# Scaling a carried attention state by two plain operations, without a clamp, and rounding later weights later

## The chip, the cores and the metric

The kernel runs on one core of one Trainium2 chip. The metric is device time in microseconds (us) of that core. One more execution is taken with the hardware profiler; its rows are what the views below show. The engines are TensorE (PE, with its weight loads PEld), VectorE (DVE), ScalarE (ACT), GpSimd (POOL) and SyncE (SP), which here only issues DMAs. Every engine works through its own instructions strictly in order.

## What is computed

Three layers in a row, in float32, for 4 batches of 768 positions:

```python
# attention with a decaying state, 8 heads of 48
f = sigmoid(f_logit)
for t in range(768):
    state = f[:, :, t, :, None] * state + k[t] (x) v[t]      # 48 x 48 for each head
    y[t] = q[t] @ state
# gated layer: x = y, 384 wide
h = relu(x @ w_in);  u, v = halves(h);  v = layernorm(v)
x = (u * (w_spatial @ v + b_spatial)) @ w_out
# mixer: first over positions, then over channels
u = x + (relu(x.T @ w_tok1) @ w_tok2).T
out = u + relu(u @ w_ch1) @ w_ch2
```

The weights arrive as 64-bit floats and are rounded to float32 on the chip. Every large product is made of three matmuls on a high and a low part (`mm3`).

## The kernel before

**Attention** is cut into 32 units: 4 batches, 2 halves of 384 positions, 4 pairs of heads. A pair lies on partitions 0 to 47 and 64 to 111. In a unit (`chunked`) DVE scans the decay into `pc` (L227), clamps the three values at the ends of the chunks of 128 from below (L232), inverts them (L233), scans back from them (L234) and scales keys and queries (L237). POOL copies the chunk-end values to `pend` (L230). Each chunk then carries a state: `z` is 112x48 for the pair (L288, L290), and for TensorE it is laid out as two diagonal 48x48 blocks of a 112x112 matrix in one of four buffers `state`, multiplied by the chunk-end decay `pp`. That is done by one instruction per chunk (L277): `z`, repeated twice, times `pp`, times a mask `own` that is 1 in the two blocks. TensorE multiplies it with the queries (L302).

**Rounding.** `round_weight` makes pieces of at most 128x384: a DMA loads the 64-bit words into a `wst` buffer (3 of them), DVE takes two steps (L65, L68), ACT scales (L72), POOL adds (L73), ACT squares (L74), DVE finishes (L78), and a DMA stores the float32 piece in DRAM (L92). The pieces of `w_tok1` (wt1d, 6), `w_tok2` (wt2d, 4), `w_ch1` (wc1d, 12) and `w_ch2` (wc2d, 12) are the list `early`, 34 pieces, staged as 37 steps.

**The order.** `weave` spreads the steps of one list among those of another. The loop over b weaves batch b of the gated layer (`s1`: norm and gate; `s23`: mix and out) with the attention of batch b+1 and with a fifth of `early` at a time. After it come the gated layer of the last batch, with the splitting of the rounded weights (`split_weight`, its subtraction on POOL, L124), and then the mixer. A scheduler moves instructions within each engine by a timeline of its own, so that the order in the program is not the one that is written.

Of the kernel before, what the change touches and what calls it, by code (L numbers as in the profile page):

```python
# [8 lines left out]
F32 = mybir.dt.float32  # L9
# [4 lines left out]
ALU = mybir.AluOpType  # L14
# [4 lines left out]
def tile_kernel(ctx, tc, fkqs, v, w_in, w_sp, b_sp, w_out, w_t1, w_t2, w_c1, w_c2, out):  # L19
    nc = tc.nc  # L20
    B, S, DM = v.shape
    P = 128
    C = 128
    W = S // 2
    D = 48
    H = DM // D
    GAP = 64 - D
    NCW = W // C
    NCH = S // C
    NP = H // 2  # L30
# [10 lines left out]
    LOW = 1e-20  # L41
# [10 lines left out]
    pend = const.tile([P, B * NP, NCH], F32, name="pend")  # L52
# [76 lines left out]
    def staged(pieces):  # L129

        gens = []

        def step(n):
            if n < len(pieces):
                gens.append(pieces[n]())
            for g in gens[max(0, n - 3) : n + 1]:
                next(g, None)

        return [partial(step, n) for n in range(len(pieces) + 3)]

    def weave(main, *fillers):

        for n, m in enumerate(main):
            for fl in fillers:
                for x in fl[len(fl) * n // len(main) : len(fl) * (n + 1) // len(main)]:
                    x()
            m()
# [9 lines left out]
    def body(general):  # L157
# [37 lines left out]
            nc.gpsimd.memset(nhalf, -0.5)  # L195
        first, last = (attp.tile([P, W], F32, name=x) for x in ("first", "last"))
        states = [attp.tile([P, 128], F32, name=f"state{i}") for i in range(4)]
        own = attp.tile([P, 2, D], F32, name="own")
        for t in [first, last, own] + states:
            nc.gpsimd.memset(t, 0.0)  # L200
        for j in range(2):
            nc.gpsimd.memset(own[64 * j : 64 * j + D, j, :], 1.0)
        if general:
            pick = attp.tile([P, D + 128], F32, name="pick")
            nc.gpsimd.memset(pick, 0.0)
# [12 lines left out]
        def chunked(u, b, hf, p, fs, fkq, vt):  # L218
# [8 lines left out]
            nc.vector.tensor_tensor_scan(  # L227
                out=pc, data0=fs[:, :W], data1=first, initial=0.0, op0=ALU.mult, op1=ALU.add
            )
            nc.gpsimd.tensor_copy(pend[:, b * NP + p, n0 : n0 + NCW], pc[:, C - 1 :: C])  # L230
            ends = last[:, C - 1 :: C]
            nc.vector.tensor_scalar(out=ends, in0=pc[:, C - 1 :: C], scalar1=LOW, scalar2=None, op0=ALU.max)  # L232
            nc.vector.reciprocal(ends, ends)  # L233
            nc.vector.tensor_tensor_scan(  # L234
                out=gc[:, ::-1], data0=fs[:, W:0:-1], data1=last[:, ::-1], initial=0.0, op0=ALU.mult, op1=ALU.add
            )
# [33 lines left out]
            for c in range(NCW):  # L270
                n = n0 + c
                if n > 0:
                    zprev = zst[b, p]
                    pp = pend[:, b * NP + p, n - 1 : n]
                    now[c] = states[cnt["state"] % len(states)]
                    cnt["state"] += 1
                    nc.vector.scalar_tensor_tensor(  # L277
                        out=now[c][:112].rearrange("p (j e) -> p j e", j=2)[:, :, :D],
                        in0=zprev[:112].unsqueeze(1).to_broadcast([112, 2, D]),
                        scalar=pp[:112],  # L280
                        in1=own[:112],
                        op0=ALU.mult,
                        op1=ALU.mult,
                    )
                if n < NCH - 1:
                    z = at3.tile([P, D], F32, tag=f"z{p}", name=f"z{u}{c}")
                    if n == 0:
                        nc.vector.tensor_copy(z[:112], pk[:112, c, :])  # L288
                    else:
                        nc.vector.scalar_tensor_tensor(  # L290
                            out=z[:112], in0=zprev[:112], scalar=pp[:112], in1=pk[:112, c, :], op0=ALU.mult, op1=ALU.add
                        )
                    zst[b, p] = z
# [111 lines left out]
        def s1(b, hf):  # L405
            if hf == 0:
                st1[b] = {
                    "vh": vnp.tile([P, NCH, DH], F32R, tag="vh", name=f"vh{b}"),
                    "vl": vnp.tile([P, NCH, DH], F32R, tag="vl", name=f"vl{b}"),
                }  # L410
            d = st1[b]
            d["u", hf] = us = up.tile([P, NJ, W], F32, tag="u", name=f"u{b}{hf}")

            def norm(i):
                xh, xl = xt[b, hf]
                ps = ps_m.tile([P, DH], F32, tag="m", name=f"pv{b}{hf}{i}")
                tsl = slice(i * P, (i + 1) * P)
                mm3(ps, [(xh[:, c, tsl], xl[:, c, tsl], winh[:, c, DH:], winl[:, c, DH:]) for c in range(NK)])
                r = rp.tile([P, DH], F32, tag="r", name=f"r{b}{hf}{i}")
                nc.scalar.activation(r, ps, AF.Relu)  # L420
                bs = smp.tile([P, 6], F32, tag="bs", name=f"bs{b}{hf}{i}")
                nc.vector.bn_stats(out=bs, in_=r)
                mv = smp.tile([P, 2], F32, tag="mv", name=f"mv{b}{hf}{i}")
                nc.vector.bn_aggr(out=mv, in_=bs)
                ve = smp.tile([P, 1], F32, tag="ve", name=f"ve{b}{hf}{i}")
                nc.gpsimd.tensor_scalar(out=ve, in0=mv[:, 1:2], scalar1=1e-6, scalar2=None, op0=ALU.add)
                rs = smp.tile([P, 1], F32, tag="rs", name=f"rs{b}{hf}{i}")
                nc.gpsimd.tensor_tensor(out=rs, in0=ve, in1=nhalf, op=ALU.pow)
                vf = rp.tile([P, DH], F32, tag="vf", name=f"vf{b}{hf}{i}")
                nc.vector.tensor_scalar(  # L430
                    out=vf, in0=r, scalar1=mv[:, 0:1], scalar2=rs, op0=ALU.subtract, op1=ALU.mult
                )
                s = hf * NCW + i
                nc.scalar.copy(d["vh"][:, s, :], vf)
                nc.vector.tensor_tensor(out=d["vl"][:, s, :], in0=vf, in1=f32(d["vh"][:, s, :]), op=ALU.subtract)

            def gate(j):
                xh, xl = xt[b, hf]
                ps = ps_m.tile([P, W], F32, tag="m", name=f"pu{b}{hf}{j}")
                jsl = slice(j * P, (j + 1) * P)  # L440
                mm3(ps, [(winh[:, c, jsl], winl[:, c, jsl], xh[:, c, :], xl[:, c, :]) for c in range(NK)])
                nc.scalar.activation(us[:, j, :], ps, AF.Relu)

            return [partial(norm, i) for i in range(NCW)] + [partial(gate, j) for j in range(NJ)]
# [57 lines left out]
        if not general:  # L502
# [1 line left out]
                kept[name], x = round_weight(wst, src, name)  # L504
                early += x
            early = staged(early)
        part = lambda n: early[len(early) * n // 5 : len(early) * (n + 1) // 5]
        for b in range(B - 1):
            if b:
                weave(s1(b, 0), rest)  # L510
            a, rest = s1(b, 1), []
            m, rest = s23(b)
            steps = att(half(b + 1, 0) + half(b + 1, 1))
            cut = len(steps) * len(a) // len(a + m)
            weave(a, steps[:cut], out_steps if b == 0 else part(2 * b - 1))
            weave(m, steps[cut:], part(2 * b))
        right.close()
        wr2 = ExitStack()
        w2p = wr2.enter_context(tc.tile_pool(name="w2p", bufs=1, side="right"))
# [1 line left out]
        t2h, t2l, st_b = split_weight(w2p, wst, kept["wt2"], "wt2", NT1, S, nc.gpsimd)  # L521
        c1h, c1l, st_c = split_weight(w2p, wst, kept["wc1"], "wc1", NK - 1, DC, nc.gpsimd)
        c1w = [(c1h[:, c, :], c1l[:, c, :]) for c in range(NK - 1)]
        weave(rest + s1(B - 1, 0) + s1(B - 1, 1), staged(st_a + st_b))
        conv = st_c
        mid.close()
        w2q = wr2.enter_context(tc.tile_pool(name="w2q", bufs=1, side="right"))
# [219 lines left out]
```

## Time and profile before

| | |
|---|---|
| median of 3 runs | 828.08 us (825.32 to 829.02) |
| the profiled execution | 828.73 us, its span 827.0 us |
| mean granted TensorE clock | 0.953 of full speed |
| busy share of the span | PE 93%, PEld 86%, DVE 54%, ACT 33%, POOL 29% |

The span runs from the first to the last instruction; 1.7 us of the profiled execution lie around it. A busy share is a mean over stages with different limits, so that each stage has to be read by itself. Durations of neighbours on an engine can overlap, so that what an instruction costs its engine is the time from its start to the start of the next.

### The profile page before, as it was taken

How to read it: one execution, taken by the hardware profiler on the slowest of the kernel's cores; microseconds unless marked ns; L12 is line 12 of the kernel's file. 1: busy time of each engine (PE TensorE's matmuls, PEld its weight loads, DVE VectorE, ACT ScalarE, POOL GpSimd, SP SyncE). 2: the span in 40 equal slices, each digit the busy share in tenths (PEclk: the TensorE clock that was granted, in tenths of full speed). 3: DMA queues.
4: the chain of work that ended last, by engine and by line, in shares of the span. 5: the costliest groups of instructions: out<-in, count | busy, mean ns of one | idle time of the engine just before them, and what ended most of it. 6: DMA issues, size and time to landing. Idle time of an engine off the chain costs nothing.

```text
span 827.0 us, 12669 instructions
## 1 busy us (share of the span) xinstructions
PE 765.1 (93%) x4785; PEld 707.5 (86%) x4785; DVE 443.2 (54%) x916; ACT 274.6 (33%) x590; POOL 240.0 (29%) x290
## 2 busy tenths in 40 slices
PE   3468698999989999999999999999999999999996
PEld 2357577787778888899899999999999999999996
DVE  6997979989898874864464352122122212222211
ACT  4554535445452433323552341112112311111110
POOL 5786835535471112110580340004001210001000
PEclk9659689999989999999999999999999999999999
DMA  7473446575644331120341230002000200000000
GB/s 240 132 219 112 146 127 207 169 255 181 220 132 149 107 104 39 58 82 23 117 134 48 87 115 30 1 1 86 1 29 1 86 1 29 1 1 31 3 28 33
DMA packets 39846, 73.67 MB, mean 89 GB/s; under 512 B 5216, under 2 KB 29664, under 8 KB 39776
## 3 DMA queue, kind: packets, MB, share of 16 engines
q1 hardware_dynamic: 39776, 72.77, 27.7%
q8 instruction: 40, 0.66, 0.3%
q14 instruction: 30, 0.25, 0.1%
HBM read 54.66 MB, written 15.73 MB: 85 GB/s over the span
## 4 chain that ended last, share of the span: by engine, by line
PE 66%; DVE 17%; DMA 6%; issue 5%; POOL 2%; ACT 1%; SPq 1%; DVEq 0%; POOLq 0%; ACTq 0%
PE po L644 18%; PE p L155 8%; PE p L153 8%; PE p L154 8%; PE ps L153 2%; PE ps L155 2%; PE ps L154 2%; PE pa L252 2%; DVE pg L227 2%; PE px L153 2%; PE px L154 2%; PE py L302 2%; PE px L155 2%; PE py L308 1%; DVE state L277 1%
## 5 line engine op out<-in xcount | busy, mean ns | idle before, releaser
L632 DVE SCALAR_TENSOR_TENSOR hl<-p,hh 128x384 fp32r<-128x384 f32 x96 | 53.4, 557 | 189.6 <-ACT hh L631 189.6
L631 ACT ACTIVATE hh<-p 128x384 fp32r<-128x384 f32 x96 | 47.1, 492 | 198.1 <-PE p L155 198.1
L644 PE MATMUL po<-hl,wc2h 128*128 128x384 f32 x288 | 97.2, 338 | 0.0
L644 PE MATMUL po<-hh,wc2l 128*128 128x384 f32 x288 | 96.7, 336 | 0.0
L655 POOL TENSOR_TENSOR us<-uh,ul 128x384 f32<-128x384 f32 x24 | 24.4, 1027 | 233.4 <-DVE ul L615 216.1
L644 PE MATMUL po<-hh,wc2h 128*128 128x384 f32 x288 | 75.0, 336 | 0.0
L153 PE MATMUL ps<-wsph,vh 128*128 128x384 f32 x192 | 66.6, 348 | 0.0
L155 PE MATMUL ps<-wsph,vl 128*128 128x384 f32 x192 | 65.9, 345 | 0.0
L154 PE MATMUL ps<-wspl,vh 128*128 128x384 f32 x192 | 65.6, 342 | 0.0
L155 PE MATMUL p<-uh,wc1l 128*128 128x384 f32 x192 | 65.0, 338 | 0.0
L154 PE MATMUL p<-ul,wc1h 128*128 128x384 f32 x192 | 64.7, 337 | 0.0
L153 PE MATMUL p<-uh,wc1h 128*128 128x384 f32 x192 | 64.2, 338 | 0.0
L257 POOL TENSOR_SCALAR_AFFINE_SELECT am<-am 128x384 f32<-128x384 f32 x64 | 42.9, 686 | 58.9 <-ACT am L256 58.7
L644 PEld LDWEIGHTS po<-hl,wc2h 128*128 128x128 f32 x288 | 54.1, 188 | 0.0
L644 PEld LDWEIGHTS po<-hh,wc2l 128*128 128x128 f32 x288 | 54.1, 188 | 0.0
L644 PEld LDWEIGHTS po<-hh,wc2h 128*128 128x128 f32 x288 | 52.3, 188 | 0.0
L302 PE MATMUL py<-fkq,state 112*112 112x128 f32 x160 | 37.4, 332 | 13.4 <-DVE state L277 10.9
L302 PEld LDWEIGHTS py<-fkq,state 112*112 112x112 f32 x160 | 26.6, 201 | 23.0 <-DVE state L277 15.9
L252 PE MATMUL pa<-fkq 48*128 48x128 f32 x384 | 40.7, 328 | 0.0
L615 DVE TENSOR_TENSOR ul<-p,uh 128x384 fp32r<-128x384 f32 x24 | 13.4, 557 | 47.6 <-ACT uh L614 47.6
L252 PEld LDWEIGHTS pa<-fkq 48*128 48x128 f32 x384 | 30.7, 215 | 9.0 <-issue 5.1
L153 PE MATMUL pu<-xh,winh 128*128 128x384 f32 x96 | 34.9, 364 | 3.6 <-ACT r L420 2.8
(407 smaller groups left out, 1944.2 us busy)
## 6 DMA issues: line engine op xcount, KB each, us to landing
fkq<-in_fkq SPq DMA_DIRECT2D x31, 576.0 KB, 4.5
vt<-in_v SPq DMA_DIRECT2D x8, 576.0 KB, 6.2
x1d<-xs SPq DMA_DIRECT2D x24, 192.0 KB, 2.0
xf<-x1d SPq DMA_DIRECT2D x12, 384.0 KB, 4.1
out<-ot SPq DMA_DIRECT2D x24, 192.0 KB, 2.5
wspsa<-in_w_sp SPq DMA_DIRECT2D x12, 192.0 KB, 3.2
wc1d<-wc1da SPq DMA_DIRECT2D x12, 192.0 KB, 2.0
wc2d<-wc2da SPq DMA_DIRECT2D x12, 192.0 KB, 2.1
```

The costliest lines, as they stand in the source:

```text
L153: nc.tensor.matmul(ps, lh, rh, start=first and i == 0, stop=False, **kw)
L154: nc.tensor.matmul(ps, lh, rl, start=False, stop=False, **kw)
L155: nc.tensor.matmul(ps, ll, rh, start=False, stop=i == n - 1, **kw)
L227: nc.vector.tensor_tensor_scan(out=pc, data0=fs[:, :W], data1=first, initial=0.0, op0=ALU.mult, op1=ALU.add)
L252: nc.tensor.matmul(pa[j][:, c, :], ki[64 * j : 64 * j + D, sl], qi[64 * j : 64 * j + D, sl], start=True, stop=True)
L257: nc.gpsimd.affine_select(out=am[j], in_=am[j], compare_op=ALU.is_ge, fill=0.0, base=0, pattern=[[0, NCW], [1, C]], channel_multiplier=-1,)
L302: nc.tensor.matmul(py[:112, c, :], now[c][:112, :112], qi[:112, c * C : (c + 1) * C], start=c == 0, stop=False, skip_group_check=True,)
L615: nc.vector.tensor_tensor(out=ul[:, c, tsl], in0=ps, in1=f32(uh[:, c, tsl]), op=ALU.subtract)
L631: nc.scalar.activation(hh, ps, AF.Relu)
L632: nc.vector.scalar_tensor_tensor(out=hl, in0=ps, scalar=0.0, in1=f32(hh), op0=ALU.max, op1=ALU.subtract)
L644: nc.tensor.matmul(po[c], l[:, ft, csl], r, start=ft == 0 and x == 0, stop=ft == NF - 1 and x == 2)
L655: nc.gpsimd.tensor_tensor(out=us[c], in0=f32(uh[:, c, tsl]), in1=f32(ul[:, c, tsl]), op=ALU.add)
```

## The change

Three things are changed. The state is laid out by two `tensor_scalar` instructions, one for each 48x48 block, in place of one over 112x2x48 with a mask; the mask `own` goes. The clamp (L232) goes, and the reciprocal reads the scan directly. The copy to `pend` is made by ACT instead of POOL. And `early` is dealt out in fourteenths: nothing in the round of b=0, 2/14 and 3/14 in that of b=1, 2/14, 2/14 and 3/14 in that of b=2, and the last 2/14 beside the gated layer of the last batch.

```diff
-        own = attp.tile([P, 2, D], F32, name="own")
-        for t in [first, last, own] + states:
+        for t in [first, last] + states:
             nc.gpsimd.memset(t, 0.0)
-        for j in range(2):
-            nc.gpsimd.memset(own[64 * j : 64 * j + D, j, :], 1.0)
...
-            nc.gpsimd.tensor_copy(pend[:, b * NP + p, n0 : n0 + NCW], pc[:, C - 1 :: C])
-            ends = last[:, C - 1 :: C]
-            nc.vector.tensor_scalar(out=ends, in0=pc[:, C - 1 :: C], scalar1=LOW, scalar2=None, op0=ALU.max)
-            nc.vector.reciprocal(ends, ends)
+            nc.scalar.copy(pend[:, b * NP + p, n0 : n0 + NCW], pc[:, C - 1 :: C])
+            nc.vector.reciprocal(last[:, C - 1 :: C], pc[:, C - 1 :: C])
...
-                    nc.vector.scalar_tensor_tensor(
-                        out=now[c][:112].rearrange("p (j e) -> p j e", j=2)[:, :, :D],
-                        in0=zprev[:112].unsqueeze(1).to_broadcast([112, 2, D]),
-                        scalar=pp[:112],
-                        in1=own[:112],
-                        op0=ALU.mult,
-                        op1=ALU.mult,
-                    )
+                    for j in range(2):
+                        r = slice(64 * j, 64 * j + D)
+                        nc.vector.tensor_scalar(
+                            out=now[c][r, r], in0=zprev[r], scalar1=pp[r], scalar2=None, op0=ALU.mult
+                        )
...
-        part = lambda n: early[len(early) * n // 5 : len(early) * (n + 1) // 5]
+        part = lambda n, m: early[len(early) * n // 14 : len(early) * m // 14]
         for b in range(B - 1):
             if b:
-                weave(s1(b, 0), rest)
+                weave(s1(b, 0), rest, part(7 * b - 9, 7 * b - 7) if b > 1 else [])
...
-            weave(a, steps[:cut], out_steps if b == 0 else part(2 * b - 1))
-            weave(m, steps[cut:], part(2 * b))
+            weave(a, steps[:cut], out_steps if b == 0 else part(7 * b - 7, 7 * b - 5))
+            weave(m, steps[cut:], part(7 * b - 5, 7 * b - 2) if b else [])
...
-        weave(rest + s1(B - 1, 0) + s1(B - 1, 1), staged(st_a + st_b))
+        weave(rest + s1(B - 1, 0) + s1(B - 1, 1), staged(st_a + st_b), part(12, 14))
```

**On DVE.** These rows stand where unit 103 (batch 1, first half, last pair) carries its state and unit 111 is scanned; a scan is listed as SCALAR_TENSOR_TENSOR writing `pg`. Before:

```order
L277 SCALAR_TENSOR_TENSOR state2_126<-z1030_1369,pend_64,own_128 112x2x48
L290 SCALAR_TENSOR_TENSOR z1031_1372<-z1030_1369,pend_64,pk103_1361 112x48
L226 MEMSET fs111_1429 128x4
L467 TENSOR_TENSOR gl000_1292<-g000_1288,gh000_1291 128x384
L68 SCALAR_TENSOR_TENSOR wc1da0768_2355<-wc1d0768st_2356,wc1da0768_2355 128x384
L78 SCALAR_TENSOR_TENSOR wc1da0384_2311<-wc1d0384st_2312,wc1da0384_2311 128x384
L277 SCALAR_TENSOR_TENSOR state3_127<-z1031_1372,pend_64,own_128 112x2x48
L290 SCALAR_TENSOR_TENSOR z1032_1375<-z1031_1372,pend_64,pk103_1361 112x48
L227 SCALAR_TENSOR_TENSOR pg111_1431<-fs111_1429,first_122 128x384
```

And after the change, with the lines of the changed program (L274 is the new state, L282 the `z` that was L290, L228 the reciprocal):

```order
L274 TENSOR_SCALAR state2_126<-z1030_1375,pend_64 48x48 x2
L282 SCALAR_TENSOR_TENSOR z1031_1379<-z1030_1375,pend_64,pk103_1367 112x48
L224 SCALAR_TENSOR_TENSOR pg111_1439<-fs111_1437,first_122 128x384
L65 TENSOR_SCALAR wc1da0768_2987<-wc1d0768st_2988 128x384
L454 TENSOR_TENSOR g002_1428<-ps002_1409,bb_495 128x384
L459 TENSOR_TENSOR gl001_1364<-g001_1360,gh001_1363 128x384
L274 TENSOR_SCALAR state3_127<-z1031_1379,pend_64 48x48 x2
L282 SCALAR_TENSOR_TENSOR z1032_1383<-z1031_1379,pend_64,pk103_1367 112x48
L228 RECIPROCAL last_123<-pg111_1439 128x3
```

Two state instructions stand together in place of one, the clamp is gone, and the weight pieces stand a little further back.

**On POOL and ACT.** The copy of the chunk ends of unit 111 stood here on POOL, in front of rounding steps:

```order
L257 AFFINE_SELECT am1100_1447<-am1100_1447 128x384
L257 AFFINE_SELECT am1101_1448<-am1101_1448 128x384
L230 COPY pend_64<-pg111_1431 128x3
L73 TENSOR_TENSOR wc1da01152_2412<-wc1da01152_2412,wc1d01152st_2413 128x384
L73 TENSOR_TENSOR wc1da10_2506<-wc1da10_2506,wc1d10st_2507 128x384
```

It now stands on ACT, with a rounding step, the copies of unit 110's scores (`am`) and more behind it (lines of the changed program):

```order
L458 CAST gh001_1363<-g001_1360 128x384
L74 ACTIVATE wc1d0384st_2911<-wc1d0384st_2911 128x384
L240 COPY kn110_1450<-pt110_1447 128x224
L227 COPY pend_64<-pg111_1439 128x3
L72 ACTIVATE wc1d01152st_3051<-wc1d01152st_3051 128x384
L251 COPY am1100_1454<-pa1100_1452 128x384
L251 COPY am1101_1455<-pa1101_1453 128x384
```

What follows the copy on ACT now waits for the scan of unit 111 as the copy does.

**The last pieces.** On POOL beside the gated layer of the last batch there are three rounding steps of `w_ch2` after the change that were all done earlier before (`wt1l` and `wt2l` are the low parts of split weights):

```order
L124 TENSOR_TENSOR wt1l_4253<-wt1sa30_4378,wt1h_4252 128x256
L73 TENSOR_TENSOR wc2da90_4306<-wc2da90_4306,wc2d90st_4307 128x384
L418 TENSOR_SCALAR ve302_4406<-mv302_4404 128x1
L124 TENSOR_TENSOR wt1l_4253<-wt1sa40_4416,wt1h_4252 128x256
L420 TENSOR_TENSOR rs302_4408<-ve302_4406,nhalf_63 128x1
L124 TENSOR_TENSOR wt1l_4253<-wt1sa50_4431,wt1h_4252 128x256
L73 TENSOR_TENSOR wc2da100_4387<-wc2da100_4387,wc2d100st_4388 128x384
```

The third of them (wc2da110) stands five rows on. In both programs the other 31 pieces stand on DVE ahead of the scan of unit 210 (batch 2, second half), where before all 34 did.

## Rows read from the trace of the kernel before

**Rows 1.** The page: busy tenths in 40 slices of the span, granted clock.

```profile
PE   3468698999989999999999999999999999999996
DVE  6997979989898874864464352122122212222211
PEclk9659689999989999999999999999999999999999
```

**Rows 2.** Busy time by stretch: stretch, length, each engine's busy time (instructions), clock, DMA.

```profile
0.00:250.00 250.00, 196.68 (x1300) 160.81 (x1301) 224.16 (x470) 122.51 (x273) 141.46 (x172) 0.85 0.57 179
250.00:390.00 140.00, 139.66 (x1032) 121.66 (x1031) 94.55 (x232) 47.70 (x106) 23.88 (x49) 1.00 0.25 80
390.00:470.00 80.00, 78.77 (x440) 76.07 (x439) 35.88 (x58) 32.35 (x69) 32.86 (x37) 1.00 0.30 93
470.00:827.00 357.00, 349.96 (x2018) 348.95 (x2017) 88.62 (x157) 72.01 (x143) 41.77 (x34) 1.00 0.09 29
```

**Rows 3.** Waits of TensorE, 250 to 390 us: total, times, longest.

```profile
PE py L302 <- DVE state L277: 0.3, 1, 0.3
```

**Rows 4.** Waits of TensorE, 390 to 470 us.

```profile
PE pu L153 <- ACT r L420: 1.2, 1, 1.2
```

**Rows 5.** Waits of all engines, 0 to 250 us.

```profile
POOL pend L230 <- DVE pg L227: 23.3, 12, 4.1
...
PEld py L302 <- DVE state L277: 15.2, 17, 2.6
...
DVE first L225 <- ACT fs L369: 12.4, 4, 4.0
```

**Rows 6.** Line 277 (state) alone, by stretch: its time on DVE (instructions).

```profile
0.00:250.00 250.00, 23.20 (x46) 0.85 0.57 179
250.00:390.00 140.00, 11.29 (x34) 1.00 0.25 80
```

**Rows 7.** Line 232 (clamp) alone, by stretch, on DVE.

```profile
0.00:250.00 250.00, 8.22 (x20) 0.85 0.57 179
250.00:390.00 140.00, 2.10 (x12) 1.00 0.25 80
```

**Rows 8.** Line 230 (copy to pend) alone, first stretch, on POOL.

```profile
0.00:250.00 250.00, 8.17 (x20) 0.85 0.57 179
```

**Rows 9.** Lines 65, 68, 78 (DVE) and 73 (POOL) alone, first stretch.

```profile
0.00:250.00 250.00, 21.96 (x47) 0.85 0.57 179
...
0.00:250.00 250.00, 26.47 (x47) 0.85 0.57 179
...
0.00:250.00 250.00, 29.86 (x47) 0.85 0.57 179
...
0.00:250.00 250.00, 56.63 (x47) 0.85 0.57 179
```

**Rows 10.** DVE by line, 250 to 390 us: shapes, count, busy us, mean ns, idle before.

```profile
L290 DVE SCALAR_TENSOR_TENSOR z<-z,pend,pk 112x48 f32<-112x48 f32 x26 | 6.7, 256 | 0.2 <-PE pk L267 0.2
...
L288 DVE COPY z<-pk 112x48 f32<-112x48 f32 x5 | 1.0, 198 | 0.5 <-PE pk L267 0.5
```

**Rows 11.** Single lines: duration ns min/median/max, first and last start.

```profile
L232 DVE TENSOR_SCALAR last<-pg x32: 154/169/993, 5.3 to 369.6; 128x3 f32<-128x3 f32 x32
...
L65 DVE TENSOR_SCALAR wc1da<-wc1d00st x1: 346/346/346, 139.4 to 139.4; 128x384 uint32<-128x384 uint32 x1
```

**Rows 12.** Timeline of DVE around 122 us: start us, duration us, what.

```profile
121.50 0.31 DVE L277 SCALAR_TENSOR_TENSOR state<-z,pend,own 112x96 f32<-112x96 f32 x1
121.73 0.25 DVE L290 SCALAR_TENSOR_TENSOR z<-z,pend,pk 112x48 f32<-112x48 f32 x1
121.90 0.41 DVE L78 SCALAR_TENSOR_TENSOR wt1da<-wt1d40st,wt1da 128x256 f32<-128x256 f32 x1
```

**Rows 13.** Timeline of POOL and DVE around 147 us.

```profile
146.69 1.48 POOL L73 TENSOR_TENSOR wc1da<-wc1da,wc1d0384st 128x384 uint32<-128x384 uint32 x1 [4.67 <-ACT wc1d0768st L72]
...
147.22 1.07 DVE L277 SCALAR_TENSOR_TENSOR state<-z,pend,own 112x96 f32<-112x96 f32 x1
148.21 0.25 DVE L290 SCALAR_TENSOR_TENSOR z<-z,pend,pk 112x48 f32<-112x48 f32 x1
```

**Rows 14.** ACT by line, 250 to 390 us.

```profile
L245 ACT COPY kn<-pt 128x224 f32<-128x224 f32 (+1 forms) x12 | 4.5, 378 | 5.9 <-PE pt L243 5.9
```

## The prediction

> **What bounds the kernel now.** Read first the page's 40 slices [rows 1]. TensorE is full from about the thirteenth slice on; before that it has holes, its granted clock is often below full, and it is DVE that stands at 9 tenths. So the kernel has two regimes, and an edit on DVE counts only in the first. The busy times by stretch give it numbers [rows 2]: from 0 to 250 us DVE is busy 224.16 of 250 us and TensorE 196.68; from 250 to 390 us it is the other way round, TensorE 139.66 of 140 and DVE 94.55; from 390 us to the end TensorE is busy for 428.73 of 437 us. TensorE's waits agree: between 250 and 390 us its matmuls wait 0.3 us in all for another engine [rows 3], between 390 and 470 us 1.2 us [rows 4], while in the first stretch its weight loads alone wait 15.2 us for the carried state [rows 5]. What the change does to DVE's time before 250 us is therefore what it does to the kernel, times about 0.9 (224.16 of 250), because DVE idles for the other tenth. Behind 250 us an edit on DVE has 45 us of cover.
>
> One more thing must be seen in that first stretch: DVE and POOL hinder each other. The same state instruction takes 11.29/34 = 0.33 us in the second stretch, where POOL is busy 23.88 of 140 us, and 23.20/46 = 0.50 us in the first, where POOL is busy 141.46 of 250 [rows 2, 6]. One of 1.07 us ends as POOL's instruction ends, and the `z` behind it, which reads PSUM, takes its usual 0.25 [rows 13]. So 46 x 0.17 = 7.9 us are lost on state instructions to POOL.
>
> **The change, part by part (first stretch).** What an instruction costs DVE is from its start to the next start. State at 121.50 and `z` at 121.73: 0.23 us for a duration of 0.31. An independent neighbour starts 0.08 before its predecessor ends, here and at 121.90 [rows 12].
>
> *State.* No row shows a 48x48 `tensor_scalar`. The one over 128x3 takes 0.154 at its shortest, the one over 128x384 takes 0.346 undisturbed [rows 11]: 0.0005 us a column, so 0.177 for 48. Neither has a scalar read from memory; `z` has one (and a second input) and takes 0.256, where the copy of the same 112x48 takes 0.198 [rows 10]: 0.058 more. Estimate 0.235, less the overlap 0.155, twice 0.31 against 0.23 now: +0.08 x 46 = **+3.7 us**. Bounds: each as short as the 128x3 one, 0.075 from start to start, gives 0.15 for two, -3.7 us; no overlap at all gives 0.47 for two, +11.0 us. I take the overlapped value, since the nearest row, state and `z`, both reading the same `z`, overlaps.
>
> *Its collisions with POOL.* Two instructions can each meet POOL; the second loses between nothing and again 7.9 us. If the two overlap, POOL has little room between them, and a first one that waited starts just when POOL has finished. I take half, **+4.0**.
>
> *Clamp.* 8.22 us for 20 instructions [rows 7], many of which collide with the copy on POOL that starts at the same scan's end. Where something independent follows, 0.08 of each was overlapped (at most 1.6 in all); where the reciprocal follows, the gap goes too. **-8.0**, between -6.6 and -8.9.
>
> *Rounding.* In the order the pieces move little: 31 of 34 still stand ahead of unit 210's scan, which DVE reaches near the end of the first stretch. Three leave it. A piece costs DVE (21.96 + 26.47 + 29.86)/47 = 1.67 us, less three overlaps 1.43 [rows 9]: **-4.3**. Their DMAs, loads and stores on SP, and their ACT and POOL steps go with them.
>
> *The copy to pend.* POOL is rid of 8.17 us here [rows 8] and of three rounding steps of 56.63/47 = 1.2 us. A POOL instruction can hold DVE for its own length at most, so the copies give between 0 and -8.2; the share that collides is some quarter (the state loses 0.17 against a mean POOL step of 141.46/172 = 0.82), **-2.0**. ACT takes 20 copies of less than 0.38 us, the time of a 128x224 copy [rows 14]; it is idle for half the stretch [rows 2], so its time costs nothing. If ACT were full, it would be up to 7.6 us.
>
> Sum on DVE: 3.7 + 4.0 - 8.0 - 4.3 - 2.0 = **-6.6**, times 0.9 **-5.9 us** of the kernel.
>
> **Behind 250 us.** 34 states add 34 x 0.08 = 2.7 us to a DVE with 45 us to spare, and 12 clamps give 2.1 back [rows 7]: nothing. The three late pieces put 3 x 1.2 = 3.6 us on a POOL that is busy 32.86 of the 80 us from 390 us on [rows 2], in front of the norms' small POOL steps, for which DVE and then TensorE wait. TensorE waits 1.2 us there now [rows 4]; I add +0.4, bounds 0 and 3.6. The mask's memsets at the start lie beside the first loads: nothing.
>
> The profiled execution took 828.73 us, 0.65 above the median and inside the spread of the runs: 828.73 - 5.9 + 0.4 = **823.2 us**.
>
> **Rivals.**
>
> *The two halves do not overlap.* All DVE instructions of this trace start at partition 0; the second half of the new state starts at 64 and the `z` behind it at 0 again. If a change of the start partition makes DVE finish what is under way, the 0.08 of overlap is lost twice for each state: 46 x 0.16 = +7.4. DVE then gains nothing, 3.7 + 7.4 + 4.0 - 14.3 = +0.8, times 0.9 and with the 0.4: **829.8 us**. No row speaks for or against it. The Trainium skill, "VectorE: DVE Perf Modes", section "Two Vector instructions with no wait between them", states just such a rule for this chip: an instruction that starts in another group of 32 partitions than the one ahead is held until every earlier one is finished. By that rule the sum would end at this rival's time and not at mine; no run here shows it yet.
>
> *ACT becomes the queue that stands still (slower).* POOL waited 23.3 us in the first stretch for scans that its copy needs [rows 5]. This wait moves to ACT, whose sigmoids, score copies and evictions stand behind it, as the order of unit 111 shows. If half of it comes back as idle time on DVE, 11.6 us are added: 823.2 + 11.6 = **834.8 us**. Against it: ACT has half its time free, and DVE's order puts other work between a scan and what needs the ACT work behind the copy. It decides when DVE's waits for ACT, now 12.4 us for the sigmoids [rows 5], rise by more than 5.5 us; by 9.0 more it is slower by half a per cent.
>
> *The state is no dearer under POOL.* The second half never collides (no +4.0) and the copies had all stood in DVE's way (-8.2, not -2.0): -16.8 x 0.9 + 0.4, **814.0 us**. For it: clamp and copy start together at each scan's end.
>
> *The gain is given back behind 390 us*, where the late pieces delay the norms, and so TensorE, by their whole 3.6 us: 828.73 - 5.9 + 3.6 = 826.4 us. For it: POOL's order there; against it: TensorE has matmuls of the batch before to run.
>
> **How the numbers follow.** My case 0.38, no overlap 0.27, ACT 0.18, cheap state 0.13, given back 0.04. A run of this kernel tells apart about half a per cent, 4.1 us, so from 823.9 to 832.2 us counts as the same. My case sits just beyond that line: I give 0.24 of it to faster and 0.14 to the same. No overlap: 0.02 faster, 0.20 the same, 0.05 slower. ACT: 0.04 the same, 0.14 slower. Cheap state: 0.13 faster. Given back: 0.03 the same, 0.01 faster. Together 0.40 faster, 0.41 the same, 0.19 slower. The likeliest single case remains mine, alone within 819 to 827 us. The range for all, 815 to 834 us, cuts off about half of the cheap state and half of ACT.
>
> **What would show it.** In the profile after: the new state line's duration (0.235 by me) and, in the timeline, whether its second half and the `z` behind it start 0.08 before or at the end of what is ahead; the state's time per chunk in the first stretch (now 0.50 us; by me two of 0.24 and 0.17 to 0.34 of collisions); DVE's waits for `fs` and ACT's for `pg`; three `wc2da` steps after 390 us and TensorE's waits there; and where TensorE becomes full, about 6 us earlier. I am wrong if that point does not move, or if it moves and the time does not.

## The result: slower by 1.1 per cent

The changed kernel takes 835.53 us (median of 4 runs, 835.12 to 836.25) against 827.15 for the kernel before, run on the same chip: ratio 1.0111, 95% interval 1.0094 to 1.0127. That is above the forecast range. Its profiled execution took 836.25 us, its span 834.2. Of all executions below, one stands apart: one of the six of e2 took 1470.31 us, and e2's median and ratio are those of the other five.

The page of the changed kernel, the slices of [rows 1]:

```profile
PE   3469698898989999999989999999999999999996
...
DVE  6998988999989774675555252222122312122211
...
PEclk9999688988989999999999999999999999999999
```

Busy time by stretch after the change, columns as in [rows 2]:

```profile
0.00:250.00 250.00, 199.09 (x1280) 163.81 (x1281) 227.94 (x484) 123.89 (x286) 130.13 (x144) 0.90 0.56 176
250.00:390.00 140.00, 138.98 (x1017) 120.90 (x1017) 101.50 (x254) 50.62 (x120) 20.92 (x38) 1.00 0.26 81
390.00:470.00 80.00, 76.55 (x432) 73.35 (x431) 39.82 (x66) 31.20 (x65) 34.30 (x37) 1.00 0.29 91
```

The two regimes stand as before. POOL has 11.3 us less to do in the first stretch, but DVE is busy for 227.94 us and not for less. The waits there, after the change, answer to [rows 5]:

```profile
ACT pend L227 <- DVE pg L224: 20.0, 15, 3.9
PEld py L294 <- DVE state L274: 19.0, 19, 2.9
...
DVE first L222 <- ACT fs L361: 8.6, 3, 3.9
```

TensorE's loads wait longer for the state (19.0 us against 15.2), DVE less for the sigmoids (8.6 against 12.4). The new state line alone, by stretch, answers to [rows 6]:

```profile
0.00:250.00 250.00, 36.58 (x92) 0.90 0.56 176
250.00:390.00 140.00, 17.85 (x68) 1.00 0.26 81
```

The timeline of DVE after the change, in a window that holds only the first half of a state, and then in a wider one in which the halves are merged into one row (x2):

```profile
121.75 0.39 DVE L68 SCALAR_TENSOR_TENSOR wt1da<-wt1d50st,wt1da 128x256 uint32<-128x256 uint32 x1
122.06 0.23 DVE L274 TENSOR_SCALAR state<-z,pend 48x48 f32<-48x48 f32 x1
...
122.06 0.49 DVE L274 TENSOR_SCALAR state<-z,pend 48x48 f32<-48x48 f32 x2
122.58 0.27 DVE L282 SCALAR_TENSOR_TENSOR z<-z,pend,pk 112x48 f32<-112x48 f32 x1
122.76 0.82 DVE L422 TENSOR_SCALAR vf<-r,mv,rs 128x512 f32<-128x512 f32 x1
```

The first half starts 0.08 us before the row ahead ends. The second can't have: a half lasts 0.23 and the two last 0.49, so that nothing overlaps and some 0.01 to 0.03 us lies empty between them. `z` starts 0.03 after the second. Behind `z` an overlap of 0.09 is back (122.76 against 122.85). From state to `z` it is 0.52 us, where it was 0.23 [rows 12]. To the nanosecond of the trace, wherever the two halves stand next to each other (76 times) the second starts 0.014 to 0.016 us after the end of the first, and a `z` that stands behind them mostly 0.032 after the end of the second.

TensorE waits in the stretch from 390 to 470 us, after the change, answer to [rows 4]; the second row had no like before:

```profile
PE pu L153 <- ACT r L412: 2.1, 1, 2.1
...
PE ps L153 <- ACT u L434: 1.3, 1, 1.3
```

**A mark in the program.** One small matmul, `row`, stands on TensorE between the third batch's last product and the norm of the last batch; its start tells where the change's first part ends. Before and after:

```profile
394.31 0.27 PE L544 MATMUL row<-ident,least 128*1 128x128 f32 x1
```

```profile
398.65 0.27 PE L536 MATMUL row<-ident,least 128*1 128x128 f32 x1
```

Taken from the time of the profiled execution it leaves 828.73 - 394.31 = 434.42 us behind the mark before, and 836.25 - 398.65 = 437.60 after: of 7.52 us lost, 4.34 are lost ahead of the mark and 3.18 behind it. Between the medians 8.4 us are lost (835.53 - 827.15).

### The profile page after: what moved, and what is told of

Read it like the earlier page. It is cut to its first block, busy times and chain, and to the rows that moved or that the text cites. A ratio compares the mean times of both kernels' runs of the same rounds, so it can differ in the third digit from the quotient of the medians.

```text
span 834.2 us, 12686 instructions
## 1 busy us (share of the span) xinstructions
PE 771.4 (92%) x4785; PEld 713.7 (86%) x4785; DVE 459.8 (55%) x964; ACT 281.1 (34%) x622; POOL 229.5 (28%) x255
## 4 chain that ended last, share of the span: by engine, by line
PE 66%; DVE 17%; DMA 7%; issue 5%; SPq 2%; POOL 1%; ACT 1%; DVEq 0%; ACTq 0%; POOLq 0%
PE po L636 18%; PE p L155 8%; PE p L153 8%; PE p L154 8%; PE ps L153 3%; DVE state L274 3%; PE ps L155 3%; PE ps L154 3%; DVE pg L224 2%; DMA fkq<-in_fkq 2%; PE px L153 2%; PE px L155 2%; PE py L300 2%; PE pa L247 2%; PE px L154 1%
## 5 line engine op out<-in xcount | busy, mean ns | idle before, releaser
L252 POOL TENSOR_SCALAR_AFFINE_SELECT am<-am 128x384 f32<-128x384 f32 x64 | 47.5, 758 | 111.2 <-ACT am L251 110.8
L274 DVE TENSOR_SCALAR state<-z,pend 48x48 f32<-48x48 f32 x160 | 54.4, 340 | 1.9
L247 PE MATMUL pa<-fkq 48*128 48x128 f32 x384 | 43.6, 334 | 0.0
L247 PEld LDWEIGHTS pa<-fkq 48*128 48x128 f32 x384 | 32.8, 219 | 9.9 <-issue 5.8
L153 PEld LDWEIGHTS ps<-wsph,vh 128*128 128x128 f32 x192 | 36.9, 192 | 3.8 <-ACT u L434 1.7
```

What stands on the lines that cost most here:

```text
L153: nc.tensor.matmul(ps, lh, rh, start=first and i == 0, stop=False, **kw)
L247: nc.tensor.matmul(pa[j][:, c, :], ki[64 * j : 64 * j + D, sl], qi[64 * j : 64 * j + D, sl], start=True, stop=True)
L252: nc.gpsimd.affine_select(out=am[j], in_=am[j], compare_op=ALU.is_ge, fill=0.0, base=0, pattern=[[0, NCW], [1, C]], channel_multiplier=-1,)
L274: nc.vector.tensor_scalar(out=now[c][r, r], in0=zprev[r], scalar1=pp[r], scalar2=None, op0=ALU.mult)
```

## The experiments

Each ratio is to runs of the kernel before on the same chip, whose median was 825.96 to 827.32 us. The mark is that of the profiled execution, the last column the profiled time less the mark. The profiled execution of before stands 1.6 us above the median of its runs here, so that the marks can be read to about 2 us. The granted clock does not make such differences: of the 103 executions of the kernel before that stand beside e1 to e18, the 27 with a mean clock below 0.967 have a median of 827.1 us, the others of 826.4. Behind the mark it is 434.1 to 436.1 us in all kernels without late rounding pieces, and 437.0 to 438.4 in all six that have them.

| kernel | median | ratio (interval) | mark | behind it |
|---|---|---|---|---|
| before | | | 394.31 | 434.42 |
| changed | 835.53 | 1.0111 (1.0094 to 1.0127) | 398.65 | 437.60 |
| e1 changed, one state operation | 830.03 | 1.0047 (1.0030 to 1.0065) | 391.02 | 438.40 |
| e2 before, two state operations | 840.21 | 1.0168 (1.0147 to 1.0189) | 405.27 | 435.93 |
| e3 before, rounding later | 827.35 | 1.0024 (1.0008 to 1.0041) | 389.19 | 437.04 |
| e4 before, no clamp, copy on ACT | 828.74 | 1.0029 (1.0015 to 1.0043) | 392.60 | 436.08 |
| e5 changed, halves from partition 0 | 827.41 | 1.0011 (0.9995 to 1.0028) | 392.17 | 437.01 |
| e6 before, no clamp | 825.93 | 1.0003 (0.9985 to 1.0020) | 391.25 | 434.38 |
| e7 before, copy on ACT | 833.74 | 1.0090 (1.0067 to 1.0114) | 398.35 | 435.95 |
| e8 e3 without late pieces | 826.69 | 1.0002 (0.9987 to 1.0017) | 392.07 | 434.58 |
| e9 e7, copy behind `kn` | 830.98 | 1.0053 (1.0032 to 1.0074) | 393.87 | 434.81 |
| e10 e9, no clamp | 832.74 | 1.0062 (1.0041 to 1.0083) | 398.62 | 434.99 |
| e11 e10, rounding later | 831.95 | 1.0064 (1.0043 to 1.0085) | 394.01 | 437.96 |
| e12 changed, copy on POOL | 835.55 | 1.0105 (1.0084 to 1.0127) | 399.92 | 437.51 |
| e13 before, fkq loads by POOL | 832.55 | 1.0071 (1.0048 to 1.0094) | 399.64 | 434.35 |
| e14 before, fkq loads by ACT | 824.38 | 0.9980 (0.9965 to 0.9995) | 389.29 | 434.11 |
| e15 e13, no clamp | 833.28 | 1.0075 (1.0050 to 1.0101) | 399.56 | 434.08 |
| e16 e13, copy on ACT | 839.16 | 1.0145 (1.0119 to 1.0171) | 404.86 | 434.40 |
| e17 e8, fkq loads by ACT | 825.21 | 0.9989 (0.9973 to 1.0005) | 390.99 | 434.38 |
| e18 e5, no late pieces, loads by ACT | 832.91 | 1.0075 (1.0053 to 1.0098) | 398.59 | 434.94 |

### The parts of the change: e1 to e4

Theory: the two halves don't overlap. Rival: ACT's queue stands still at the copy. Each part alone, or all but the state:

```diff
# e1, to the changed kernel (e2, to the kernel before: the reverse)
-                        nc.vector.tensor_scalar(
-                            out=now[c][r, r], in0=zprev[r], scalar1=pp[r], scalar2=None, op0=ALU.mult
-                        )
+                    nc.vector.scalar_tensor_tensor(
+                        out=now[c][:112].rearrange("p (j e) -> p j e", j=2)[:, :, :D],
...
# e3, to the kernel before: part(n, m) and its four uses as in the change
-        part = lambda n: early[len(early) * n // 5 : len(early) * (n + 1) // 5]
+        part = lambda n, m: early[len(early) * n // 14 : len(early) * m // 14]
...
# e4, to the kernel before
-            nc.gpsimd.tensor_copy(pend[:, b * NP + p, n0 : n0 + NCW], pc[:, C - 1 :: C])
-            ends = last[:, C - 1 :: C]
-            nc.vector.tensor_scalar(out=ends, in0=pc[:, C - 1 :: C], scalar1=LOW, scalar2=None, op0=ALU.max)
-            nc.vector.reciprocal(ends, ends)
+            nc.scalar.copy(pend[:, b * NP + p, n0 : n0 + NCW], pc[:, C - 1 :: C])
+            nc.vector.reciprocal(last[:, C - 1 :: C], pc[:, C - 1 :: C])
```

> The changed kernel with the state put back to one instruction with the mask; clamp gone, copy on ACT and rounding as changed. Theory 1 (the change of start partition keeps the two halves and the z behind them apart: 0.29 us more per state on DVE, 46 states before 250 us): about 823 us, faster than before by 0.5%, TensorE's last-batch mix earlier by some 10 us than in the changed kernel. Theory 2 (the copy on ACT holds its queue up): still 833 us or more. Theory 3 (the late rounding pieces): the 2.6 us that the changed kernel loses between 390 and 430 us are lost here too, whatever the rest does.

> The kernel before with nothing but the two-instruction state. Theory 1: DVE is charged 46 x 0.29 = 13 us before 250 us and nothing is given back, so 836 to 840 us, slower than the changed kernel or equal to it. Theory 2: within 0.3% of before. Theory 3: the same, within 0.3% of before.

> The kernel before with nothing but the rounding pieces dealt out later. Theory 1: three pieces leave the first stretch, about 4 us saved there, and the stretch behind 390 us may take some back: 823 to 828 us. Theory 3 (late pieces stand in POOL's and ACT's queues beside the last gated layer): TensorE loses 2.6 us between 390 and 430 us, net 827 to 830 us.

> The kernel before with the clamp gone and the copy of the chunk ends on ACT, one state instruction, rounding as before. Theory 1: DVE is rid of 8 us before 250 us: 820 to 823 us. Theory 2 (ACT's queue stands still for the scans): 831 us or more, with DVE's waits for the sigmoids above the 12.4 us of before.

The state alone costs 1.68 per cent, 14 us: more than the whole change. The state line of e2, by stretch:

```profile
0.00:250.00 250.00, 37.60 (x88) 0.94 0.55 174
250.00:390.00 140.00, 17.90 (x68) 1.00 0.28 88
```

The rounding and the two edits at the scan's ends, which were to gain, lose a quarter of a per cent each. The rounding's mark comes 5.1 us earlier, but behind the mark it loses 2.6. Of the 5.1, some 3.7 are scatter: the profiled execution of before stands 2.6 above the median of e3's chip, that of e3 1.1 below its own.

e1 takes 830 us where theory 1 had 823. These two edits do add up: 0.24 and 0.29 per cent, and 0.47 for both in e1. It is the state that does not: 14 us alone, and in the changed kernel only 835.53 - 830.03 = 5.5 us. Why it is cheaper there is not shown.

### The start partition alone: e5

```diff
+            for j in range(2):
+                r = slice(64 * j, 64 * j + D)
+                nc.scalar.copy(half_ends[r, j, b * NP + p, n0 : n0 + NCW], pc[r, C - 1 :: C])
...
-                            out=now[c][r, r], in0=zprev[r], scalar1=pp[r], scalar2=None, op0=ALU.mult
+                            out=now[c][:112, 64 * j : 64 * j + D], in0=zprev[:112],
+                            scalar1=half_ends[:112, j, b * NP + p, n - 1 : n], scalar2=None, op0=ALU.mult,
```

Two operations still, of 48 columns each, but both over 112 partitions from partition 0; `half_ends` holds the chunk ends with zeros in the other head's rows.

> The changed kernel with each of the two state instructions over 112 partitions from partition 0 (112x48), scaled by a column of chunk ends that holds zeros for the other half; ACT makes two more small copies per unit for these columns. As many state instructions with as many columns as in the changed kernel, but none changes the start partition. Theory 1 (the change of start partition): neighbours overlap by 0.08 us again, state to state about 0.16 us instead of 0.25, the pair and z 0.2 us cheaper per state, some 9 us before 250 us: 826 to 830 us, near the version with one state instruction (830 us). Rival 1b (it is the number of instructions, not where they start): 835 us as the changed kernel, and 0.25 us from start to start.

It is back at the time of before, 8.1 us below the changed kernel, with two copies more for ACT in each unit. Up to one and the same instruction (TensorE's first transpose for unit 212: batch 2, second half, third pair) the changed kernel and then e5 show

```profile
0.00:280.10 280.10, 229.19 (x1503) 190.45 (x1504) 253.22 (x548) 133.54 (x310) 134.34 (x150) 0.91 0.54 169
```

```profile
0.00:274.00 274.00, 225.50 (x1500) 187.21 (x1501) 243.03 (x544) 140.84 (x358) 135.32 (x151) 0.93 0.55 173
```

so 10.2 us less on DVE, and the point 6.1 earlier. The timeline of DVE in e5:

```profile
252.35 0.39 DVE L277 TENSOR_SCALAR state<-z,half_ends 112x48 f32<-112x48 f32 x2
252.66 0.25 DVE L286 SCALAR_TENSOR_TENSOR z<-z,pend,pk 112x48 f32<-112x48 f32 x1
252.95 0.40 DVE L277 TENSOR_SCALAR state<-z,half_ends 112x48 f32<-112x48 f32 x2
```

The two last 0.39 us together, and `z` starts 0.08 before they end: 0.31 from state to `z`, where the changed kernel has 0.52. The state line of e5, by stretch:

```profile
0.00:250.00 250.00, 30.84 (x94) 0.92 0.57 181
250.00:390.00 140.00, 14.38 (x66) 1.00 0.23 71
```

Busy time counts a stretch in which two overlap once: so a half comes to 0.218 us in the second stretch here and to 0.263 in the changed kernel. Single ones are as long in both, as the view of the one line shows (shortest, median and longest in ns), of e5 and of the changed kernel:

```profile
L277 DVE TENSOR_SCALAR state<-z,half_ends x160: 211/242/1067, 17.8 to 382.6; 112x48 f32<-112x48 f32 x160
```

```profile
L274 DVE TENSOR_SCALAR state<-z,pend x160: 207/247/1034, 17.2 to 389.4; 48x48 f32<-48x48 f32 x160
```

The start partition is shown as the cause of the 0.21 us. In e5 the second operation overlaps the first by 0.076 to 0.092 us wherever the two stand next to each other (79 times), though both write one tile there too. Nor is it the height: in the changed kernel the first half, of 48 partitions, overlaps the row of 128 ahead of it by 0.08. How much of the 8.1 us of the kernel it makes is less sharp. The program's order on DVE differs between the two kernels in other places as well, and e5 is 2.6 us faster than e1, whose single state operation costs DVE 0.08 us less.

### Clamp and copy apart, and the rounding without its late pieces: e6 to e8

e6 takes the clamp away and e7 puts the copy on ACT, each alone in the kernel before. e8 is e3 with the last 2/14 moved up:

```diff
-            weave(m, steps[cut:], part(7 * b - 5, 7 * b - 2) if b else [])
+            weave(m, steps[cut:], part(7 * b - 5, 7 * b - 2 if b < 2 else 14) if b else [])
...
-        weave(rest + s1(B - 1, 0) + s1(B - 1, 1), staged(st_a + st_b), part(12, 14))
+        weave(rest + s1(B - 1, 0) + s1(B - 1, 1), staged(st_a + st_b))
```

> The kernel before without the clamp, the copy of the chunk ends still on POOL, nothing else. If the 8 us of the clamp on DVE are real: 819 to 822 us. Rival 2b (the clamp only stood where POOL's copy held DVE anyway, so the wait moves on to the next instruction that needs the shared way to SBUF): 825 to 828 us, and the scan back or its neighbours are longer by what the clamp no longer waits.

> The kernel before with nothing but the copy of the chunk ends moved from POOL to ACT. Theory 2 (ACT's queue stands still for the scans): 830 to 834 us, so that with the clamp's saving the two come to the 829 us that they measured together. Rival: 824 to 827 us, POOL being rid of 8 us.

> The kernel before with the rounding dealt out as changed but for the last 2/14, which go into the round of b=2 with the rest; all 34 pieces then stand ahead of unit 210's scan again. Theory 3 (three pieces less before 250 us give some 3 us and cost some 2.6 us behind 390 us): both vanish, 825 to 828 us, and TensorE loses nothing between 390 and 430 us. Rival: the gain came from the spacing of the pieces, not from the three that leave, and without the late ones it is 823 us.

Taken from the kernel before, the clamp is worth nothing that can be measured. DVE is indeed rid of it: up to the first transpose for unit 212 the kernel before and e6 show

```profile
0.00:277.90 277.90, 224.24 (x1516) 184.59 (x1516) 246.46 (x528) 130.35 (x291) 145.62 (x180) 0.86 0.55 173
```

```profile
0.00:273.10 273.10, 223.58 (x1500) 186.48 (x1501) 241.29 (x500) 131.45 (x290) 149.65 (x179) 0.94 0.55 176
```

so 246.46 - 241.29 = 5.2 us less on DVE and the point 4.8 earlier; at the mark 3.1 are left, and of these 1.6 are the scatter of the profiled execution of before. With the copy on ACT right behind the scan the clamp is worth something: e4 is e7 without it and takes 5.0 us less. The copy alone costs 0.9 per cent. ACT's wait for the scan and a new wait of DVE stand in e7's first stretch:

```profile
ACT pend L230 <- DVE pg L227: 11.9, 12, 2.2
...
DVE first L225 <- ACT fs L369: 9.2, 4, 3.9
...
DVE state L277 <- PE py L302: 7.0, 2, 5.2
```

DVE's wait for the sigmoids is no longer than before; what is new are 7.0 us in which it waits for TensorE to give a state buffer back.

Moved up, the late pieces cost nothing behind the mark: 434.58 us there, against 437.04 in e3. TensorE's waits from 390 to 470 us in e3, and then in e8:

```profile
PE ps L153 <- ACT u L442: 2.0, 1, 2.0
...
PE pu L153 <- ACT r L420: 1.5, 1, 1.5
```

```profile
PE pu L153 <- ACT r L420: 1.2, 1, 1.2
```

The wait of the last batch's mix is there only with the late pieces, in five of the six kernels that have them; e5 lacks it and still takes 437.01 us behind the mark, so that the wait does not explain all of this cost. And e8's mark is 2.9 us later than e3's.

### Is it ACT's standing wait: e9 to e12

In e9 the copy stands behind that of `kn`, whose zero column is its bias, so that what it waits for is long done. e10 is e9 without the clamp, e11 adds the rounding as changed; e12 is the changed kernel with the copy back on POOL.

```diff
-            nc.gpsimd.tensor_copy(pend[:, b * NP + p, n0 : n0 + NCW], pc[:, C - 1 :: C])
...
             nc.scalar.copy(kn[:, :ncs, :], pt[:, :ncs, :])
+            nc.scalar.activation(
+                pend[:, b * NP + p, n0 : n0 + NCW], pc[:, C - 1 :: C], AF.Identity, bias=kn[:, 0, D : D + 1]
+            )
```

> The kernel before with the copy of the chunk ends on ACT, but with a zero column of the transposed keys (kn) as its bias, so that it stands right behind the copy of kn and never waits for the scan. Theory 2 (on ACT the copy's wait for the scan holds up the copies, sigmoids and evictions behind it, which is the 0.9% of the version that only moves the copy): ACT's waits for pg vanish from the list and the time is 825 to 829 us. Rival 2c (ACT does not lose by the wait, but the order that the scheduler makes around the copy is worse): 831 to 834 us again, without any wait of ACT for pg.

> The same with the clamp gone. The clamp's removal gave nothing with the copy on POOL (825.9 against 827.1) and some 5 us with the copy on ACT (828.7 against 833.7). If its 7 us on DVE are real and TensorE only takes a part of them: 820 to 825 us. Rival (the removal is worth what ACT's standing queue took): no more than the version before it, 825 to 829 us.

> The changed kernel with one state instruction and the copy on ACT behind kn. Theory 1 and 2 together: everything that cost is gone, 820 to 825 us, of which the late rounding pieces take 2 to 3 us behind 390 us. Rival: 828 to 830 us as with the copy right behind the scan.

> The changed kernel with the copy of the chunk ends back on POOL: two state instructions, no clamp, rounding as changed. Theory 2: 0.5 to 0.9% faster than the changed kernel, 829 to 832 us. Rival 2c: within 0.3% of the changed kernel, 833 to 837 us.

In e9 no wait of ACT's copy for the scan is left, and it still loses 0.5 of the 0.9 per cent. Taking the clamp away on top gives nothing (e10), nor does the rounding (e11): both came out above what either theory had. And in the changed kernel the copy's engine makes no difference: e12 is as slow, with POOL waiting for the scan in place of ACT. So a queue that stands still at this copy explains at most a part of its cost.

### Late loads: e13 to e18

Half of DVE's idle time in the first stretch is for the sigmoids (12.4 of 25.8 us), and ACT there waits for the loads of `fkq`, which stand in SP's queue behind the loads and stores of the rounding. Theory: what DVE saves is lost again to these loads. But SP also stands at the loads themselves, until TensorE gives a buffer back; the kernel before, 0 to 250 us:

```profile
SPq L361 <- PE py L302: 18.7, 7, 8.7
```

Another queue does not by itself bring that buffer earlier.

```diff
# e13, e15 (no clamp as well), e16 (copy on ACT as well)
-                nc.sync.dma_start(out=fkq, in_=fkqs[b, p, hf])
+                nc.gpsimd.dma_start(out=fkq, in_=fkqs[b, p, hf])
# e14, e17 (on e8), e18 (on e5, with the late pieces moved up as in e8)
+                nc.scalar.dma_start(out=fkq, in_=fkqs[b, p, hf])
```

> The kernel before, with the loads of a unit's keys, queries and decays (fkq) started by GpSimd in place of SyncE, whose queue also holds the rounding's loads and stores and waits for them in order. Theory (late loads take back what DVE saves): ScalarE's wait for fkq (15.2 us before 250 us in the kernel before) falls below 5 us and with it DVE's wait for the sigmoids (12.4 us); the time falls by 3 to 6 us, to about 822. Rival (DVE's idle time only stands where TensorE's other waits are): within 0.3 per cent of the kernel before. Third way: the loads wait on GpSimd for a free buffer and hold the score masks back, 1 per cent slower.

> The same loads started by ScalarE. Theory: as with GpSimd, about 3 to 6 us faster, if ScalarE's queue doesn't stand still for a free buffer. Rival: ScalarE stands still at each load until TensorE's product of three units before is done; then DVE's wait for the sigmoids rises above 20 us and the time by 1 per cent or more.

> The loads started by GpSimd, and the clamp gone. Theory (late loads ate the clamp's credit): 5 to 7 us below the run with the loads moved alone. Rival (a DVE instruction of 0.2 to 0.4 us in this place stands in idle time anyway): within 2 us of it.

> The loads started by GpSimd, and the copy of the chunk ends on ScalarE. The copy alone cost 0.9 per cent, and ScalarE's longest wait for fkq was 6.6 us there against 3.4. Theory (its loss was a late load): within 2 us of the run with the loads moved alone. Rival (ScalarE's queue itself): 5 to 8 us above it.

On POOL the loads lose 0.7 per cent. In the first stretch ACT waits 10.3 us for them (15.2 before) and DVE 5.6 for the sigmoids (12.4 before), so that shorter waits there did not make the kernel faster. POOL stands still at the loads, between 250 and 390 us in e13 and in e16:

```profile
POOL fkq L361 <- PE py L302: 13.4, 7, 4.5
```

```profile
POOL fkq L361 <- PE py L302: 38.3, 8, 8.0
```

For e13 this is not where the time is lost: TensorE is busy for all of these 140 us, but for only 190.37 us of the first 250 (196.68 before). There starting a load takes POOL 0.56 us, 11.8 us for 20; that these make the loss is not shown. The clamp is worth nothing in this kernel either (e15), and the copy costs 6.6 us in it (e16), as in the kernel before. With the loads on ACT (e14) the kernel is 0.2 per cent faster, the only one of all that stands below 1 with its interval; but ACT's waits for the loads didn't shorten in the first stretch (15.2 us before):

```profile
ACT fs L369 <- DMA fkq<-in_fkq: 22.1, 9, 4.2
...
DVE first L225 <- ACT fs L369: 9.9, 6, 6.0
```

So the gain of e14 is there and isn't explained by the theory. Nor is the theory refuted: no run made the loads punctual (in e15 ACT waits 18.7 us for them). The last two:

> The kernel before with two of the edits that did no harm: the loads of fkq started by ScalarE (alone 0.2 per cent faster) and the rounding dealt out as changed, with its last two fourteenths in the round of b=2 (alone no change). Theory (the rounding's gain of 2 to 3 us up to 390 us is real and adds): 2 to 3 us below the loads alone, ratio 0.994 to 0.996. Rival (DVE's credits are taken back whichever they are): within 1 us of the loads alone, 0.998.

> The changed kernel mended: both halves of the state start at partition 0, the last pieces of the rounding are done in the round of b=2, the loads of fkq are started by ScalarE. Theory (what cost the time was the restart at another partition and the late pieces; clamp and copy are worth nothing): as the run above, 0.994 to 0.998. Rival (ScalarE's queue cannot hold the copy to pend, the zeroed copies and the loads too): 1.003 or more.

e17 is no faster than e14. e18 adds two edits that did no harm elsewhere to e5 and stands 5.5 us above it, as its rival had it; whether it is ACT's queue, which there holds the copies and the loads, or another order was not taken apart. Edits of a microsecond are followed on this kernel by shifts of several, of either sign.

## Why the prediction was wrong

**The regimes: right.** What e2 loses it loses ahead of the mark (11.0 of 12.5 us of the profiled executions), and behind 250 us the 34 dearer states of the changed kernel cost TensorE 0.7 us of its busy time at most (138.98 against 139.66 in [rows 2]).

***State: wrong, the step that failed.*** "I take the overlapped value, since the nearest row, state and `z`, both reading the same `z`, overlaps." That row has two instructions that start at the same partition, the new ones don't. That all instructions of the old trace start at partition 0 stood in the prediction's own rival; the sum left it out. The operation itself was priced right (0.235 by the prediction, 0.23 measured). From state to `z` it is 0.52 us, not 0.31: +0.29 x 46 = +13.3 us in place of +3.7, above the bound of +11.0 as well, since that let neighbours touch and here 0.015 to 0.03 lies between them. e5, which starts both at partition 0, has 0.31, the value of the sum. What the kernel pays for this depends on what else is in it: 0.29 x 46 x 0.9 = 12.0 us by the prediction's factor, and 14.0 measured alone (e2) but 5.5 in the changed kernel (against e1); 0.21 x 46 x 0.9 = 8.7, and 8.1 measured (against e5). The Trainium skill's page "VectorE: DVE Perf Modes", section "Two Vector instructions with no wait between them", had the rule: an instruction that starts in another group of 32 partitions is held until those ahead are finished. The trace agrees, with 0.015 to 0.03 us of gap where 0.08 of overlap was, twice for each state.

***Collisions: right.*** A half lasts 36.58/92 = 0.398 us in the first stretch and 17.85/68 = 0.263 in the second: 0.135 x 92 = 12.4 us, 4.5 more than the 7.9 of before. The sum had +4.0. (The row of 1.07 us in [rows 13] ends at 148.29, 0.12 after POOL's, and not with it.)

***Clamp: the work right, its worth wrong.*** Some 5 us leave DVE up to the same instruction (e6), but -8.0 x 0.9 = -7.2 was not had: e6 is at 1.0003, the interval's lower end 1.2 us below no change. The factor 0.9 takes every microsecond of DVE for one of the kernel's. That held nearly for the state in two of three comparisons and for the clamp only beside the copy on ACT (e4 against e7, 5.0 us), not in three others (e6; e10 against e9; e15 against e13). Where the credit goes was not settled.

***Rounding: the gain too large, what comes back too small.*** Between e8 and e3 the three pieces move the mark by 2.9 us in the profiled executions, against -4.3 x 0.9 = -3.9. Behind the mark they cost 2.5 us (e3 against e8), not 0.4: more than half of the 3.6 of the rival that gives all back, which had a chance of 0.04. By the medians e3 stands 0.22 per cent, 1.8 us, above e8, which leaves a gain of only 0.7. The mix of the last batch waits (e3, 2.0 us; the changed kernel, 1.3).

***Copy: wrong in sign.*** Alone it costs 6.6 us (e7) where -2.0 was forecast. The ACT rival had foreseen a loss, but by DVE's waits for sigmoids; these fell from 12.4 to 8.6 us, its own sign didn't show, and more than half of the loss stays without the standing wait (e9), while in the changed kernel there is none (e12). Its cause stays open; that the scheduler's order is behind it was not shown.

***The rivals.*** "No overlap" named the cause, and at 829.8 us was too cheap by 5.7: it let the halves touch without a gap and kept the credits of clamp and copy, which did not come. With the measured state (+9.6 x 0.9 = 8.6) and late pieces (+2.2 to 2.8) the sum comes to 823.2 + 11 = 834 us. That it comes so close is luck, since it still holds -9.0 us for clamp and copy, which together cost 2.4 (e4): with that it would be some 845 us, 10 too many. So too for the parts measured alone: they add up to 1.68 + 0.24 + 0.29 = 2.2 per cent, twice what the whole change costs. Why they cost less together stays open. The ACT rival's 834.8 us is nearer still, but without its sign.

## What to carry to other kernels

Before splitting one DVE instruction into two by partition range, look where each starts: on another partition than its neighbours, every switch cost the overlap and a gap here (partitions 0 and 64), some 0.1 us, nearly half of the length of these small instructions. The same two instructions can be had from partition 0, with zeros where the other half was masked. And a microsecond off a busy engine need not be worth one: 5 us less of DVE's work gave nothing here. Its worth is to be forecast from zero up to the full microsecond, and a single edit is to be measured in the kernel that it is meant for, since the same edit cost 14 us in one and 5.5 in the other.

## What was not expected of the hardware

The gap of 0.015 to 0.03 us at a change of the start partition, where an independent instruction from the same partition starts 0.08 before the end of the one ahead. e2 has it like the changed kernel:

```profile
255.97 0.49 DVE L276 TENSOR_SCALAR state<-z,pend 48x48 f32<-48x48 f32 x2
256.50 0.26 DVE L284 SCALAR_TENSOR_TENSOR z<-z,pend,pk 112x48 f32<-112x48 f32 x1
```

And more partitions cost next to nothing: the shortest 48-column operation takes 211 ns over 112 partitions (e5) and 207 over 48.
